# Attention plus gated MLP on one core: PV in batches of eight, zero matmuls at the start, two key segments, denominators by DMA

## The chip, the cores and the metric

The kernel runs on one core of one Trainium2 chip. The metric is device microseconds (us) of an execution. A run of several executions is given as its median. The clock of TensorE in the records is a share of full speed. Only two values of it occur, 0.5 and 1.0, and a mean such as 0.90 says that a fifth of the time was spent at half clock.

On one core a run is labelled slow when it took over 1.5% longer than the fastest run of the same kernel.

Names: TensorE (PE) multiplies matrices, ScalarE (ACT) computes exp and tanh, VectorE (DVE) copies and multiplies elementwise, GpSimd (POOL) does the same more slowly (one layer norm operation of 128x448 takes 1.41 us there and 0.33 us on VectorE, in the profile of before). PSUM is the memory that matmuls write to.

## The reference

```python
# x: 1 x 2048 x 448, bf16; 16 heads of 28; MLP width 1792
xn  = layernorm(x)
qkv = xn @ wqkv                        # 448 x 1344
p   = softmax(q @ k.T * 28**-0.5)      # 16 heads, 2048 x 2048
A   = (p @ v) @ wo
B   = (gelu_tanh(xn @ w_gate) * (xn @ w_up)) @ w_down
out = x + A + B
```

## The kernel before

The scores of one head are computed transposed, keys on partitions. A *unit* is one head, one chunk of 128 keys and one block of 512 queries: one 128x512 score matmul and one PV matmul. There are 4 query blocks x 16 heads x 16 key chunks = 1024 units, three to an exp, so 342 *steps*. Each step emits, in this order, the exp of step p on ScalarE, the three score matmuls of step p+2 on TensorE (two score buffers in PSUM), some PV matmuls, and at most about one *slot*. A slot is a group of four or five matmuls of everything else: projections, V, gate and up, the down and output projections.

```python
spool  = tile_pool(name="spsum",  bufs=2, space=PSUM)   # scores, 3 banks each
otpool = tile_pool(name="otpsum", bufs=1, space=PSUM)   # PV accumulator, 1 bank
aux    = tile_pool(name="aux",    bufs=1, space=PSUM)   # every slot: 1 bank
...
for p in range(NP):                                     # 342 steps
    emit_exp(p)                                         # ScalarE, 128 x 1536
    if tanh_q and tanh_q[0][0] <= p:
        tanh_q.pop(0)[1]()                              # 28 times in all
    if p + 2 < NP:
        emit_s(p + 2)                                   # three score matmuls
    pv_q.extend(units_of(p))
    n = 0
    while pv_q and n < (4 if len(pv_q) > 4 else 3):     # PV: three or four per step
        ...
        emit_pv(pv_q.pop(0)); n += 1
        ...                                             # end of a block: evict, queue g_norm
    ...
    if credit[0] >= 1.0 or due_now or p >= END:
        slots.append(run_slot())                        # one slot
    ...
    for s in evs: s[2]()                                # VectorE empties the slot's bank
```

The softmax denominators come out of the PV matmul as row 0 of each head's 32 rows (V carries a column of ones). Before, they were gathered and spread with matmuls, in 16 normalisations:

```python
def g_norm(Q, hg, otsb, beng=nc.gpsimd):
    ps = aux.tile([P, 16], F32, tag="a", name="dn")
    for ch in range(TPQ):                               # 4 fp32 matmuls, recorded as 8
        nc.tensor.matmul(ps[:, 4*ch:4*ch+4], lhsT=otsb[:, ch*P:(ch+1)*P], rhs=selc[:], ...)
    def f_rec():
        nc.vector.reciprocal(rec[:], ps[:])
        beng.tensor_copy(recx[:], rec[:].unsqueeze(2).to_broadcast([P, 16, 32]))
    yield ("evac", 250, f_rec)
    bt = aux.tile([P, QT], F32, tag="a", name="bt")
    for ch in range(TPQ):
        nc.tensor.matmul(bt[:, ch*P:(ch+1)*P], lhsT=recx[...], rhs=ident[:], ...)
    ...
```

A block runs over all 16 key chunks of four heads, so the first 22 steps already need K and V of every token:

```python
def unit(u):
    return u // 256, (u // 64) % 4, (u // 4) % 16, u % 4   # query block, head group, key chunk, head
```

The softmax here doesn't subtract the row's maximum and nothing guards it: scores larger than these inputs give would overflow.

## Time and profile before

The median is 634.89 us over three runs, 628.87 to 637.83. The profiled execution spans 621.2 us. It is a separate execution of 623.05 us, faster than all of these: the stage table below shows before near its best.

| stage (profile of before) | us | ScalarE's floor | lost |
|---|---|---|---|
| head, until the first exp | 23.2 | | |
| first block, 86 exps | 188.3 | 119.2 | 69 |
| rest, 256 exps | 396.4 | 366.4 | 30 |
| tail, after the last exp | 13.3 | | |

The floor is what ScalarE needs if it never waits. Where exps run back to back in the timeline (near 600 us) they start every 1.342 us, and a tanh adds 0.95 us, so the first block with its four tanh needs 86 x 1.342 + 4 x 0.95 = 119.2 us, and the rest 256 x 1.342 + 24 x 0.95 = 366.4 us.

The page in 40 slices, of before: each digit is the busy share of a slice of 15.5 us in tenths, and PEclk is the granted clock in tenths.

```profile
PE   2477878999989989999999999999898999999874
ACT  1433465869968999999999899998999899999791
PEclk9999996578977999899979799989999799999665
```

ScalarE is nearly full from the fourteenth slice on, and mostly far from full before it.

The busy time of each engine in the four stages, of before. The columns are the stretch in us, its length, the busy time of the five engines with the number of instructions, the mean clock, the DMA share and GB/s.

```profile
0.00:23.20 23.20, 6.91 (x30) 3.18 (x31) 15.08 (x38) 4.70 (x8) 13.07 (x22) 1.00 0.70 173
23.20:211.60 188.40, 159.71 (x827) 50.59 (x826) 70.04 (x129) 125.12 (x92) 40.97 (x62) 0.86 0.10 28
211.60:607.90 396.30, 368.16 (x2361) 129.31 (x2359) 158.56 (x267) 372.38 (x279) 8.43 (x12) 0.93 0.09 27
607.90:621.20 13.30, 5.13 (x20) 2.52 (x16) 4.56 (x8) 0.02 (x1) 0.00 (x0) 0.50 0.10 35
```

The waits of before: who waited for whom, us in total, how often, the longest.

```profile
ACT e L443 <- PE st L429: 86.1, 90, 5.0
...
PE st L429 <- ACT e L443: 18.9, 40, 4.0
...
PE gups L282 <- DVE gu L331: 0.5, 2, 0.2
```

Exps (`e`) wait 86 us for scores (`st`). The view counts waits over 0.15 us.

The timeline of before, one full step in the rest: start in us, duration, engine, line, operation, and in brackets the idle time before it.

```profile
363.71 0.39 PE L429 MATMUL st<-qT,kT_176 28*128 28x512 bf16 x3
...
364.04 0.40 PE L454 MATMUL ot<-e,vaug 128*32 128x512 bf16 x3
...
364.36 0.93 PE L373 MATMUL op<-wd_sb,ht 128*128 128x448 bf16 x4
...
365.23 0.39 PE L429 MATMUL st<-qT,kT_176 28*128 28x512 bf16 x3
```

Score, PV and slot follow each other without a gap: 0.33 + 0.32 + 0.87 = 1.52 us, so this step is longer than the 1.342 us of an exp. Steps with a slot are limited by TensorE, steps without one by ScalarE.

### The profile page before, as it was taken

How to read it: one execution, taken by the hardware profiler on the slowest of the kernel's cores; microseconds unless marked ns; L12 is line 12 of the kernel's file. 1: busy time of each engine (PE TensorE's matmuls, PEld its weight loads, DVE VectorE, ACT ScalarE, POOL GpSimd, SP SyncE). 2: the span in 40 equal slices, each digit the busy share in tenths (PEclk: the TensorE clock that was granted, in tenths of full speed). 3: DMA queues.
4: the chain of work that ended last, by engine and by line, in shares of the span. 5: the costliest groups of instructions: out<-in, count | busy, mean ns of one | idle time of the engine just before them, and what ended most of it. 6: DMA issues, size and time to landing. Idle time of an engine off the chain costs nothing.

```text
span 621.2 us, 7981 instructions
## 1 busy us (share of the span) xinstructions
PE 539.9 (87%) x3232; PEld 185.6 (30%) x3232; DVE 248.2 (40%) x440; ACT 502.2 (81%) x378; POOL 62.5 (10%) x96
## 2 busy tenths in 40 slices
PE   2477878999989989999999999999898999999874
PEld 1122222223322333333333333332332333333321
DVE  6434232045544541155655401656546104650202
ACT  1433465869968999999999899998999899999791
POOL 7586400000000000000000000000000000000000
PEclk9999996578977999899979799989999799999665
DMA  8700000011111100021211001112111002000000
GB/s 205 198 13 0 0 1 2 0 31 30 31 30 31 31 1 16 8 82 46 60 31 31 0 16 46 48 42 60 31 30 31 8 16 61 8 1 1 0 2 30
DMA packets 33925, 20.24 MB, mean 33 GB/s; under 512 B 1568, under 2 KB 33888, under 8 KB 33888
## 3 DMA queue, kind: packets, MB, share of 16 engines
q1 hardware_dynamic: 33088, 18.87, 10.9%
q10 hardware_dynamic: 800, 0.86, 0.5%
q8 instruction: 25, 0.41, 0.3%
q14 instruction: 12, 0.10, 0.1%
HBM read 17.89 MB, written 1.84 MB: 32 GB/s over the span
## 4 chain that ended last, share of the span: by engine, by line
PE 54%; DVE 17%; ACT 17%; issue 9%; POOL 2%; DMA 1%; ACTq 0%; DVEq 0%; POOLq 0%
ACT e L443 15%; PE gups L282 14%; PE st L429 9%; PE ot L454 9%; PE op L373 9%; PE pp L237 5%; DVE gu L331 4%; PE pv L251 3%; PE dn L338 3%; DVE g L293 3%; ACT th L313 2%; DVE vaug L262 2%; DVE res L379 1%; POOL xn L202 1%; DVE qT L244 1%
## 5 line engine op out<-in xcount | busy, mean ns | idle before, releaser
L443 ACT ACTIVATE e<-st 128x1536 bf16<-128x1536 f32 x342 | 474.1, 1459 | 87.2 <-PE st L429 86.1
L454 PE MATMUL ot<-e,vaug 128*32 128x512 bf16 x1024 | 147.5, 434 | 4.4 <-DVE vaug L262 4.4
L282 PE MATMUL gups<-xnT,wg 112*128 112x512 bf16 x224 | 63.9, 412 | 3.9 <-DVE gu L331 0.5
L293 DVE CAST g<-gups 128x512 bf16<-128x512 f32 x56 | 38.7, 691 | 70.2 <-PE gups L282 70.2
L282 PE MATMUL gups<-xnT,wu 112*128 112x512 bf16 x224 | 59.3, 388 | 4.3
L454 PEld LDWEIGHTS <-vaug 128*32 128x32 bf16 x1024 | 34.0, 94 | 94.7 <-issue 83.7
L350 POOL CAST recx<-rec 128x512 bf16<-128x512 f32 x15 | 10.3, 684 | 501.9 <-DVE rec L349 501.9
L373 PE MATMUL op<-wd_sb,ht 128*128 128x448 bf16 x224 | 55.8, 371 | 0.5
L331 DVE TENSOR_TENSOR gu<-gups,g 128x512 bf16<-128x512 f32 x56 | 38.7, 691 | 34.0 <-PE gups L282 33.8
L429 PE MATMUL st<-qT,kT_176 28*128 28x512 bf16 x256 | 39.1, 442 | 8.5 <-ACT e L443 6.0
L429 PE MATMUL st<-qT,kT_179 28*128 28x512 bf16 x256 | 39.9, 438 | 6.9 <-ACT e L443 6.4
L237 PE MATMUL pp<-xnT,wqk_sb 112*128 112x512 bf16 x120 | 38.9, 456 | 5.1 <-DVE xnT L220 1.8
L429 PE MATMUL st<-qT,kT_177 28*128 28x512 bf16 x256 | 38.8, 427 | 3.3 <-ACT e L443 2.8
L429 PE MATMUL st<-qT,kT_178 28*128 28x512 bf16 x256 | 35.3, 394 | 4.6 <-ACT e L443 3.8
L379 DVE TENSOR_TENSOR res<-op,x_sb 128x448 bf16<-128x448 f32 x12 | 7.5, 624 | 70.2 <-PE op L373 70.2
L282 PEld LDWEIGHTS <-wg 112*128 112x128 bf16 x224 | 20.4, 101 | 33.4 <-issue 19.0
L313 ACT ACTIVATE th<-zz 128x1024 bf16<-128x1024 bf16 x28 | 29.7, 1061 | 0.0
L282 PEld LDWEIGHTS <-wu 112*128 112x128 bf16 x224 | 20.0, 98 | 30.7 <-issue 14.0
L373 PEld LDWEIGHTS <-ht 128*128 128x128 bf16 x224 | 19.0, 100 | 25.2 <-issue 14.1
L217 PE MATMUL tp<-ident,xn 128*112 128x128 bf16 x64 | 9.2, 317 | 18.7 <-DVE xn L202 9.8
L338 PE MATMUL dn<-selc,otsb 128*128 128x4 f32 x128 | 18.8, 270 | 7.3 <-DVE otsb L617 5.4
L251 PE MATMUL pv<-wv_sb,xnT 112*128 112x448 bf16 x64 | 21.5, 477 | 2.0 <-DVE kT_176 L244 1.6
(102 smaller groups left out, 353.8 us busy)
## 6 DMA issues: line engine op xcount, KB each, us to landing
wg<-in_B_w_gate_dram SPq DMA_DIRECT2D x28, 224.0 KB
wu<-in_B_w_up_dram SPq DMA_DIRECT2D x28, 224.0 KB
out_dram<-res SPq DMA_DIRECT2D x16, 112.0 KB
wd_sb<-in_B_w_down_dram SPq DMA_DIRECT2D x1, 1568.0 KB
x_sb<-in_A_x_dram SPq DMA_DIRECT2D x2, 448.0 KB
wst<-in_A_wqkv_dram SPq DMA_DIRECT2D x1, 392.0 KB
wst<-in_A_wqkv_dram ACTq DMA_DIRECT2D x1, 392.0 KB
wv_sb<-in_A_wqkv_dram SPq DMA_DIRECT2D x1, 392.0 KB
```

The costliest lines, as they stand in the source:

```text
L237: nc.tensor.matmul(pp[:, 0:QT] if ps is None else pp, lhsT=wqk_sb[:, comp, hg, c, :], rhs=xnT[:, c, T * QT : (T + 1) * QT], start=(c == 0) ...
L251: nc.tensor.matmul(pv[:, 0:D], lhsT=xnT[:, c, tt * P : (tt + 1) * P], rhs=wv_sb[:, c, :], start=(c == 0), stop=(c == NDC - 1),)
L282: nc.tensor.matmul(ps[:], lhsT=w[:, c, k * P : (k + 1) * P], rhs=xnT[:, c, Q * QT : (Q + 1) * QT], start=(c == 0), stop=(c == NDC - 1),)
L293: yield ("evac", C_EVAC, lambda ps=ps, k=k: nc.vector.tensor_copy(g[:, k, :], ps[:]))
L313: nc.scalar.activation(st["t"][:], st["z"][:], AF.Tanh, scale=TANH_SCALE)
L331: yield ("evac", C_EVAC, lambda ps=ps, k=k: nc.vector.tensor_mul(gu[:, k, :], ps[:], g[:, k, :]))
L338: nc.tensor.matmul(ps[:, 4 * ch : 4 * ch + 4], lhsT=otsb[:, ch * P : (ch + 1) * P], rhs=selc[:], start=True, stop=True,)
L373: nc.tensor.matmul(ps[:, 0:D], lhsT=l, rhs=r, start=(first and n == 0), stop=(last and n == len(seq) - 1))
L379: nc.vector.tensor_add(res[:], a, b)
L429: nc.tensor.matmul(st[:, j * QT : (j + 1) * QT], lhsT=kT[hg][32 * hh : 32 * hh + Dh, kc * P : (kc + 1) * P], rhs=qT[(Q, hg)][32 * hh : 32 ...
L443: nc.scalar.activation(e[:, 0:n], st[:, 0:n], AF.Exp, scale=SCALE)
L454: nc.tensor.matmul(ot_cur[0][32 * hh : 32 * hh + 32, :], lhsT=vaug[:, kc, h * 32 : (h + 1) * 32], rhs=e[:, j * QT : (j + 1) * QT], start=( ...
```

## The change

The change has four announced parts, and some smaller ones in the same diff.

1. **PV in batches of eight units.** PV is emitted only when eight units wait, every second or third step. Fewer switches between score and PV matmuls should free TensorE.
2. **Zero matmuls while inputs load.** 24 matmuls of zeros at the start and a few more in the head keep TensorE busy, so that its clock is full when the first real work comes.
3. **First query block in two key segments.** All head groups first run over key chunks 0 to 3, later over 4 to 15, and the partial results are added. The first 21 steps then need only the first four token tiles.
4. **Denominators reshaped by DMA.** Four small DMAs spread row 0 of each head over partitions, VectorE takes the reciprocal, four DMAs bring it back to a row, and one matmul broadcasts it.

Smaller: layer norm of tiles 4 to 15 goes mostly from GpSimd to VectorE and later; its evictions in the head are split; slots are admitted by an estimate of TensorE's backlog; the output stores at the end use two queues. Exp buffers go from 7 to 6.

```diff
-        n = 0
-        while pv_q and n < (4 if len(pv_q) > 4 else 3):
-            ...
+        take = 8 if len(pv_q) >= 8 else (4 if p >= NP - 4 and len(pv_q) >= 4 else 0)
+        if take and unit(pv_q[take - 1])[2] in v_done:
+            for _ in range(take):
+                u = pv_q.pop(0)
+                if emit_pv(u) and u != NU - 1:
+                    close_block(u)
... (cut)
+    SEG = 4
+    blocks = [(0, hg, 0, SEG) for hg in range(NHG)] + [(0, hg, SEG, NKC) for hg in range(NHG)]
+    blocks += [(Q, hg, 0, NKC) for Q in range(1, NQ) for hg in range(NHG)]
... (cut)
+    def norm_stage1(otsb):
+        for j in range(4):
+            nc.sync.dma_start(den[32 * j : 32 * j + 32, :], otsb[32 * j : 32 * j + 1, :])
+    def norm_stage2(den, rr):
+        nc.vector.reciprocal(rec[:], den[:])
+        nc.vector.tensor_copy(recb[:], rec[:])
+        for j in range(4):
+            nc.sync.dma_start(rr[32 * j : 32 * j + 1, :], recb[32 * j : 32 * j + 32, :])
+    def g_norm(Q, hg, otsb, rr):
+        nc.tensor.matmul(bt[:], lhsT=sel[:], rhs=rr[:], start=True, stop=True)
... (cut)
+    def junk(ps, n):
+        for _ in range(n):
+            nc.tensor.matmul(ps, lhsT=zt[:, 0:P], rhs=zt[:], start=True, stop=True)
+    jt = otpool.tile([P, QT], F32, tag="ot", name="jt")
+    junk(jt[:], 24)
... (cut)
+        if overdue or ((credit[0] >= 1.0 or p >= END) and backlog + C_SLOT <= dt + 900):
+            ev = run_slot()
```

## The prediction

> What bounds it now. ScalarE is the long pole, fed by TensorE. By the groups, 342 exps keep ScalarE busy 474 us, 28 tanh 30 us. Back to back, exps start every 1.342 us (timeline, 598-606 us), so ScalarE's floor is 342 x 1.342 + 28 x 0.95 = 485 us; the span is 621 us. The waits show ScalarE idle 86 us for score matmuls. The stretch table places the loss: first exp at 23.2 us; the first query block (86 exps) lasts until about 200 us, where 86 x 1.342 + 7 tanh is 122 us, so 55 us are lost; the other 256 exps take about 408 us against 364, so 44 us are lost; from the last exp to the end pass 13 us.
>
> TensorE causes this twice. Warm, its work nearly fills the time: 342 score groups and 334 PV batches (instruction order) of 3 or 4 matmuls at 0.32 us of issue each (four cost what three cost), about 240 slots of four or five matmuls at 0.97 us, 16 normalisations at 1.4 us: 109 + 108 + 232 + 22 = 470 us. And it is often not warm: the granted clock is 0.5 at 97-131, 178-192, 579-590 and from 597 us, and durations say the start is cold too (four K matmuls 1.86 us at 34 us, 1.02 us at 86 us), though the clock row shows 1.0 there. The cold stretches follow a 4 us slice with TensorE under 60% busy. That agrees with the Trainium skill, "TensorE: Matmul & The Clock Gate", Part 1 (half clock by default and after an idle window of about 3.4 us).
>
> What the change does.
> 1. PV by eight: 128 batches. If the switch costs 0.32 - 0.216 = 0.1 us, eight cost 2 x 0.216 + 0.1 = 0.54 us; 69 us in place of 108.
> 2. Denominators by DMA: 128 small fp32 matmuls (18.8 us busy) and 64 others become 15 single matmuls; about 20 us off TensorE, and its waits for the reciprocal go. The price, eight tiny DMAs per block, hides behind eight steps (11 us).
> Together TensorE falls to about 410 us warm, clearly under ScalarE.
> 3. Zero matmuls should warm TensorE; that and fewer operations before the first exp (layer norm of tiles 4-7 moved out, a split evacuation, earlier table load) bring it to about 16.5 us; the weight DMA at 10.3 us stays the limit.
> 4. Two key segments: the first 21 steps need only token tiles 0-3, so the rest of layer norm, transposes, K and V spreads over the block. Most of the 55 us come back.
> 5. Tail: bf16 denominators, four output banks, two store queues: 3 us less.
>
> Sum: 16.5 + 485 + 10 = 511 us if ScalarE never waited. I allow 28 us of stalls (half in the first block, half from cold stretches) and some 10 us for the clock's phase, since the runs before spread by 9 us.
>
> Predicted: 550 us, range 527 to 585. Faster by over 2%: 0.95; within 2%: 0.03; slower: 0.02.
>
> Right if: first exp before 18 us; 86th exp ends before 155 us; PV batches of eight near 0.54 us at full clock; ScalarE's idle time for score matmuls falls from 86 to under 35 us; TensorE's busy time falls by 60 us or more; ScalarE over 88% busy.
>
> Wrong if: lower TensorE load lets the clock fall to half more often (mean under 0.85), so that slots limit again; zero matmuls don't count as activity; denominator DMAs land later than four steps and block VectorE; the single auxiliary PSUM bank makes slots wait for evacuations; the layer norm of tiles 4-15 comes too late for step 22.

## More of the kernel before

Verdicts use the other runs, the fast ones.

The clock row shows half-clock stretches. Its first record lies at 76.8 us, so the nines before that are not a measurement. The matmuls themselves tell: the same V projection takes 1.68 us before the record and 0.93 us after it (timeline of before).

```profile
68.64 1.68 PE L251 MATMUL pv<-wv_sb,xnT 112*128 112x448 bf16 x4
...
78.25 0.93 PE L251 MATMUL pv<-wv_sb,xnT 112*128 112x448 bf16 x4
```

All matmuls of projection slots from 34.8 to 76.3 us start 0.33 to 0.43 us apart, and those of the first slot after 76.8 us 0.19 to 0.20. So the clock was at half there too, and of the first block not 51 us, as recorded, but some 105 us passed at half clock if the stretch from the first exp to 34.8 us was like the rest.

In the rest both engines are over 90% busy: TensorE 368 and ScalarE 372 of 396 us.

The timeline of before at a normalisation:

```profile
145.82 1.05 PE L338 MATMUL dn<-selc,otsb 128*128 128x4 f32 x8
...
147.23 0.61 POOL L350 CAST recx<-rec 128x512 bf16<-128x512 f32 x1 [48.34 <-DVE rec L349]
...
147.90 0.40 PE L355 MATMUL bt<-ident,recx 128*128 128x128 bf16 x4 [0.38 <-POOL recx L350]
...
149.15 1.89 PE L237 MATMUL pp<-xnT,wqk_sb 112*128 112x512 bf16 x4
```

Right after it, from 148.5 us on, the clock is at half, and the projection slot (`pp`) takes 1.89 us instead of 1.0.

## The result, and the profile after

The changed kernel takes 571.14 us (median of four runs, 566.59 to 577.09). Before, four runs in the same rounds give 635.09 us. The ratio of fast runs is 0.898, with a 95% interval of 0.888 to 0.908. All ratios here are the mean time of one kernel's fast runs over that of the other's fast runs of the same rounds, so they are not quite the ratios of the medians.

The prediction of 550 us lay 21 us low, and the measurement inside its range. The stages below are those of the two profiles.

| stage | before | after | difference |
|---|---|---|---|
| head | 23.2 | 19.0 | -4.2 |
| first block | 188.3 | 142.0 | -46.3 |
| rest | 396.4 | 399.0 | **+2.6** |
| tail | 13.3 | 9.6 | -3.7 |

Between the two profiles, nearly the whole gain lies in the first block. The rest, two thirds of the time, gained nothing, although TensorE is busy 31 us less there. The table accounts for 51.6 of the 64 us between the medians, because the profile of before is of an execution 12 us faster than its median; where the other 12 us lie in a usual run of before is not shown.

The page in slices (14.2 us each), of after:

```profile
PE   7768788878788999888789898878886998869775
ACT  2778879988899899999885999999989899998983
PEclk9998997998999699999875999999986899989977
```

The busy time by stage, of after:

```profile
0.00:19.00 19.00, 14.77 (x67) 5.78 (x68) 14.23 (x42) 5.50 (x9) 11.40 (x30) 1.00 0.97 212
19.00:161.00 142.00, 111.89 (x771) 36.46 (x769) 72.82 (x146) 122.24 (x91) 2.69 (x13) 0.93 0.11 28
161.00:560.00 399.00, 337.18 (x2253) 101.79 (x2252) 167.89 (x293) 371.54 (x280) 0.00 (x0) 0.91 0.11 30
560.00:569.60 9.60, 4.27 (x22) 1.32 (x18) 4.28 (x8) 0.59 (x2) 0.00 (x0) 0.86 0.15 48
```

In the rest TensorE is busy for 337 us in place of 368, but the stretch is as long as before, and its mean clock fell from 0.93 to 0.91.

The waits of after:

```profile
PE st L473 <- ACT e L487: 47.8, 71, 1.9
ACT e L487 <- PE st L473: 41.9, 66, 2.2
...
PE gups L315 <- DVE g L326: 11.9, 27, 0.5
...
PE gups L315 <- DVE gu L365: 7.8, 19, 0.5
```

TensorE now waits 48 us for ScalarE (19 before), and ScalarE still 42 us for TensorE. Each is idle for the other at different times. The last two lines are new: gate and up slots wait 46 times, 19.7 us together, for VectorE to empty their bank.

The timeline of after, one such wait:

```profile
283.76 0.69 DVE L365 TENSOR_TENSOR gu<-gups,g 128x512 bf16<-128x512 f32 x1 [0.39 <-PE gups L315]
284.16 1.45 ACT L487 ACTIVATE e<-st 128x1536 bf16<-128x1536 f32 x1
...
284.51 1.02 PE L315 MATMUL gups<-xnT_187,wu 112*128 112x512 bf16 x4 [0.46 <-DVE gu L365]
...
285.46 0.39 PE L473 MATMUL st<-qT,kT_3_1668 28*128 28x512 bf16 x3
...
285.79 0.40 PE L500 MATMUL ot<-e,va_155 128*32 128x512 bf16 x4
...
285.96 1.45 ACT L487 ACTIVATE e<-st 128x1536 bf16<-128x1536 f32 x1 [0.35 <-PE st L473]
286.01 0.39 PE L500 MATMUL ot<-e,va_156 128*32 128x512 bf16 x4
...
286.33 1.04 PE L270 MATMUL pp<-xnT_188,wqk_sb 112*128 112x512 bf16 x4
```

VectorE empties the bank until 284.45. The slot had stood ready for 0.46 us and starts at 284.51. The scores are queued behind the slot and start at 285.46, and ScalarE idles 0.35 us before the exp that needs them. The two exps start 1.80 us apart, not 1.34: the 0.46 us are passed on. The step before had a slot too and no PV in between; the eight PV matmuls come only afterwards, and take 286.33 - 285.79 = 0.54 us, as predicted.

In the head, the timeline of after shows a tiny operation that takes long:

```profile
6.25 2.41 DVE L192 CAST mvb_191<-mv_190 128x8 bf16<-128x8 f32 x1
...
7.04 1.59 POOL L122 MEMSET wo_sb<- 128x1792 bf16 x1
8.69 0.17 DVE L193 TENSOR_SCALAR ve_192<-mvb_191 128x4 bf16<-128x4 bf16 x1
```

The cast of 128 x 8 elements ends at 8.66 us, when the memset on GpSimd ends (8.63). The next operation, half its size, takes 0.17 us. In the second profile of the same kernel (a_again below) the cast ended before this memset began, and the timeline of a_again shows:

```profile
6.38 0.25 DVE L192 CAST mvb<-mv 128x8 bf16<-128x8 f32 x1
...
7.10 1.59 POOL L122 MEMSET wo_sb<- 128x1792 bf16 x1
```

### The profile page after: what moved, and what is told of

Read it like the earlier page. It is cut to its first block, busy times and chain, and to the rows that moved or that the text cites. A ratio compares the mean times of both kernels' runs of the same rounds, so it can differ in the third digit from the quotient of the medians.

```text
span 569.6 us, 7901 instructions
## 1 busy us (share of the span) xinstructions
PE 468.1 (82%) x3106; PEld 145.3 (26%) x3106; DVE 259.2 (46%) x486; ACT 499.9 (88%) x379; POOL 14.1 (2%) x43
## 4 chain that ended last, share of the span: by engine, by line
PE 44%; ACT 28%; DVE 14%; issue 12%; POOL 0%; DMA 0%; DVEq 0%; ACTq 0%; POOLq 0%
ACT e L487 24%; PE gups L315 14%; PE st L473 8%; PE ot L500 7%; PE op L407 6%; PE pp L270 5%; ACT th L346 3%; DVE gu L365 3%; PE pv L284 3%; DVE g L326 2%; DVE res L413 1%; DVE xn L235 1%; DVE qT L277 0%; DVE on L390 0%; DVE zz L341 0%
## 5 line engine op out<-in xcount | busy, mean ns | idle before, releaser
L487 ACT ACTIVATE e<-st 128x1536 bf16<-128x1536 f32 x342 | 471.1, 1477 | 47.7 <-PE st L473 41.9
L407 PEld LDWEIGHTS <-ht 128*128 128x128 bf16 x224 | 19.2, 100 | 31.3 <-issue 20.5
L519 DVE COPY otsb<-ot 128x512 f32<-128x512 f32 x12 | 8.3, 691 | 32.4 <-PE ot L500 21.3
L331 DVE TENSOR_TENSOR sq<-g 128x1024 bf16<-128x1024 bf16 x28 | 19.3, 688 | 0.4
L357 DVE TENSOR_TENSOR ht<-ph,gu 128x1024 bf16<-128x1024 bf16 x28 | 19.2, 686 | 0.4
L270 PEld LDWEIGHTS <-wqk_sb 112*128 112x128 bf16 x128 | 11.9, 104 | 29.0 <-issue 22.6
L341 DVE TENSOR_TENSOR zz<-po,g 128x1024 bf16<-128x1024 bf16 x28 | 19.2, 684 | 0.3
L315 PE MATMUL gups<-xnT_188,wg 112*128 112x512 bf16 x56 | 16.9, 432 | 2.5 <-DVE g L326 1.2
L390 DVE TENSOR_TENSOR on<-otsb,bt 128x512 bf16<-128x512 f32 x15 | 10.3, 685 | 18.3 <-PE bt L387 18.3
L315 PE MATMUL gups<-xnT_188,wu 112*128 112x512 bf16 x56 | 16.1, 415 | 2.7 <-DVE g L326 1.8
L315 PE MATMUL gups<-xnT_187,wg 112*128 112x512 bf16 x56 | 15.3, 397 | 2.9 <-DVE g L326 1.8
L315 PE MATMUL gups<-xnT_186,wg 112*128 112x512 bf16 x56 | 15.3, 397 | 2.7 <-DVE g L326 1.4
L277 DVE CAST qT<-pp 128x512 bf16<-128x512 f32 x15 | 10.4, 692 | 15.3 <-PE pp L270 15.3
L315 PE MATMUL gups<-xnT_189,wg 112*128 112x512 bf16 x56 | 14.4, 380 | 3.1 <-DVE g L326 1.4
L315 PE MATMUL gups<-xnT_186,wu 112*128 112x512 bf16 x56 | 14.4, 380 | 3.0 <-DVE g L326 1.7
L315 PE MATMUL gups<-xnT_189,wu 112*128 112x512 bf16 x56 | 15.3, 398 | 1.8 <-DVE gu L365 0.9
```

Of the source, the lines that this page charges most:

```text
L270: nc.tensor.matmul(pp[:, 0:QT] if ps is None else pp, lhsT=wqk_sb[:, comp, hg, c, :], rhs=xnT[T][:, c, :], start=(c == 0), stop=(c == NDC ...
L315: nc.tensor.matmul(ps[:], lhsT=w[:, c, k * P : (k + 1) * P], rhs=xnT[Q][:, c, :], start=(c == 0), stop=(c == NDC - 1),)
L331: nc.vector.tensor_mul(st["a"][:], g[:], g[:])
L341: nc.vector.tensor_mul(st["z"][:], st["b"][:], g[:])
L357: nc.vector.tensor_mul(ht[:], st["p"][:], gu[:])
L407: nc.tensor.matmul(ps[:, 0:D], lhsT=l, rhs=r, start=(first and n == 0), stop=(last and n == len(seq) - 1))
```

## The experiments

Twelve runs were made, of ten new kernels and two repeats, all with correct results. Kernels whose name begins with b_ start from the kernel before, those with a_ from the changed one. The two theories on the rest were:

- **Bank:** with PV in every step, its 0.32 us between two slots hid the emptying of the one bank (0.69 us). With eights, a slot often follows a slot directly and must wait.
- **Clock:** with less to do, TensorE has idle moments, the clock falls to half, and slots limit again.

### a_pv4: the changed kernel with PV in threes and fours

```diff
-        take = 8 if len(pv_q) >= 8 else (4 if p >= NP - 4 and len(pv_q) >= 4 else 0)
-        if take and unit(pv_q[take - 1])[2] in v_done:
-            for _ in range(take):
+        n = 0
+        while pv_q and n < (4 if len(pv_q) > 4 else 3):
...
```

> The changed kernel with PV put back to batches of three and four. LOAD expects 20 to 30 us more than the changed kernel (about 595 us), most of it after the first block. STAGE expects at most 10 us more (571 to 581 us), the rest of the exps within 6 us of the 399 us of the changed kernel.

Measured: 559.6 us (552.57 to 569.36), ratio to before 0.882 (0.875 to 0.890). Undoing the part that was meant to relieve TensorE made the kernel faster; both theories for this run expected it slower or the same. The profile is of the fastest of its runs (552.57 us), so it flatters a_pv4. In it the rest takes 381.2 us, 18 less than after, and TensorE is busier in it (348.3 against 337.2 us) at a mean clock of 0.97. The busy time of that stage, and two waits, of a_pv4:

```profile
159.80:541.00 381.20, 348.26 (x2251) 117.36 (x2250) 167.15 (x293) 370.60 (x280) 0.00 (x0) 0.97 0.12 31
```

```profile
PE st L473 <- ACT e L487: 28.8, 55, 1.6
...
PE gups L315 <- DVE gu L365: 0.5, 1, 0.5
```

The timeline of a_pv4, one step with PV between two slots:

```profile
171.42 0.39 PE L473 MATMUL st<-qT,kT 28*128 28x512 bf16 x3
171.52 0.69 DVE L365 TENSOR_TENSOR gu<-gups,g 128x512 bf16<-128x512 f32 x1 [0.52 <-PE gups L315]
...
171.74 0.40 PE L500 MATMUL ot<-e,va 128*32 128x512 bf16 x3
...
172.27 1.02 PE L315 MATMUL gups<-xnT,wg 112*128 112x512 bf16 x4
```

While VectorE empties the bank (171.52 to 172.21), TensorE does scores and then PV, and the slot starts without a wait in the records. In the order of the traces, 120 slots of the changed kernel follow the slot of the step before with no PV in between; in the kernel before and in a_pv4 it is 5. (The expectation of a_mix below has 98 and 3, by a count of its own.) Both theories are still standing: the bank waits went from 19.7 to under 1 us, but the clock rose too.

### a_again and a_pv4_again: both once more, on another chip

No edit.

> The changed kernel itself, unchanged, so that the next three stand beside it on the same chip. 566 to 577 us as before, granted clock about 0.91, about 100 us at half clock.

> The changed kernel with PV in threes and fours, a second time and beside the changed kernel: the first time it was faster (559.6 us; 39.9 us at half clock in its profile against 98.3, PE busy 484 against 468 us). CLOCK theory: less TensorE work leaves idle stretches, the clock falls to half, and the slots that follow run behind; so it is again 1 to 3% faster than the changed kernel, with a clock over 0.94. Rival CHANCE: the two are within 1%, the first comparison was the clock's phase.

Measured: 572.24 us (563.33 to 575.18), ratio 0.901 (0.892 to 0.910), and 565.85 us (557.16 to 571.10), ratio 0.890 (0.882 to 0.898). The order is the same, with a smaller distance, and here the intervals overlap. Over all eight runs of each, whatever their label, the means are 571.1 and 562.6 us, so eights cost 8.5 us.

The profiles of these two fell into runs labelled slow. Compared with each other they show the same as the first pair: the rest takes 397.4 us with eights and 383.3 us with threes and fours. The first block, however, takes 148.0 and 158.4 us, where the first pair had 142.0 and 142.7: in a_pv4_again 65 us of it passed at half clock, in the others 14 to 41. This is most of what makes one run of these two kernels longer than another.

### a_mix: eights, but at most four in a step after a slot

```diff
+        most = 4 if slot_last else 8
+        n = 0
+        if len(pv_q) >= 8 or (pv_q and (slot_last or p >= NP - 4)):
+            while pv_q and n < most:
...
```

This takes the bank wait away by order alone: nearly every slot after a slot gets PV in between (all but 5 in the trace). There are 251 PV batches then, in place of 128.

> The changed kernel with at most four PV matmuls in a step that follows a slot (so that PV stands between two slots), eights elsewhere: 251 PV batches in place of 128 (eights) or 336 (threes and fours). A slot that follows a slot with no PV between: 98 in the changed kernel, 3 here and 3 with threes and fours. BANK theory: slots share one PSUM bank, a slot must wait until VectorE has emptied it; PV used to hide that, batches of eight uncover it (waits of matmuls for VectorE's gate and up evictions 19.7 us in the changed kernel, none with threes and fours), and the scores behind the slot wait too. Then these waits fall below 4 us and the exps after the first block take 378 to 388 us, total 555 to 566 us. CLOCK theory: what hurts is low TensorE load; the load here is only about 11 us above that of eights, so the half clock stays near 100 us and the rest at 393 to 400 us.

Measured: 572.0 us (568.03 to 582.71), ratio 0.910 (0.904 to 0.915). The changed kernel did not run in this call, so only ratios compare, and this one is no better than its 0.898 and 0.901. In the profile the bank waits are nearly gone and the rest takes 386.2 us, 13 less than after. But the first block takes 154.5 us, with a stretch of 31 us at half clock. Two waits of a_mix:

```profile
PE gups L315 <- DVE gu L365: 2.1, 3, 1.1
...
PE gups L315 <- DVE g L326: 0.7, 2, 0.5
```

So the rest came out as the bank theory expected, but the total did not (555 to 566 us), and the half clock stayed near 100 us, as the clock theory expected. In the rest itself 31 us less passed at half clock than in after, so the 13 us are not the bank's alone. What was gained there was lost in the first block, where the clock was low.

### a_warm: eights, with zero matmuls wherever a step has room

```diff
+        fill = (0 if ran else 2) + (0 if dt == T_EXP else 3)
+        if fill and pv_open[0]:
+            for _ in range(fill):
+                nc.tensor.matmul(ot_cur[0][:], lhsT=zt[:, 0:P], rhs=zt[:], start=False, stop=False, ...)
```

Zeros are added to the open PV accumulator, so the result does not change. A step without a slot gets two, a step with a tanh three more.

> The changed kernel, PV in eights, and zero matmuls (128x512, added into the open PV accumulator, which they leave as it is) wherever a step ran no slot (2) or has a tanh (3). CLOCK theory: they keep the clock up, time at half clock falls from 98 to under 40 us, the exps after the first block take 375 to 385 us in place of 399, total 545 to 558 us. Rival BUNCH: batches of eight are slow because 0.54 us of PV in one step holds back scores; then more matmuls make it no faster: 566 to 585 us.

Measured: 565.05 us (563.11 to 568.42), ratio 0.901 (0.894 to 0.907), beside 0.901 for the changed kernel. In the profile the whole rest ran at full clock, and TensorE waited only 12.3 us for ScalarE. But the rest still takes 391.4 us and the bank waits stay at 20 us. The waits and the stage of a_warm:

```profile
PE st L473 <- ACT e L487: 12.3, 27, 1.4
PE gups L315 <- DVE g L326: 12.0, 26, 0.5
...
PE gups L315 <- DVE gu L365: 8.0, 18, 0.5
```

```profile
160.60:552.00 391.40, 356.88 (x2455) 113.22 (x2454) 168.31 (x293) 372.83 (x280) 0.00 (x0) 1.00 0.11 31
```

So the bank waits outlast the half clock. How much of the loss the clock was, this run does not show: its total is above the 545 to 558 us that the clock theory expected, but it does 202 zero matmuls more in the rest, and a_pv4_warm below shows that zeros placed by this rule can themselves cost time.

### What the four profiles say together

a_mix takes away the bank waits, a_warm the half clock, a_pv4 the bank waits and, in its profile, most of the half clock. For each profile, the idle time of ScalarE in the rest was added up from the trace: every gap over 30 ns by the clock at that moment, and at full clock by whether a slot had waited for its bank in the 2.5 us before. A gap at half clock counts as the clock's, whatever came before it. All four are profiles of fast runs.

| ScalarE idle in the rest, us | after | a_mix | a_warm | a_pv4 |
|---|---|---|---|---|
| at half clock | 12.7 | 6.7 | 0 | 1.2 |
| at full clock, after a bank wait | 5.7 | 0.2 | 10.9 | 0 |
| at full clock, other | 9.0 | 8.7 | 7.7 | 9.3 |
| sum | 27.5 | 15.6 | 18.5 | 10.5 |
| the rest, us | 399.0 | 386.2 | 391.4 | 381.2 |
| of it at half clock | 72.8 | 41.5 | 0 | 21.3 |

From after to a_pv4 the idle time falls by 17.0 us, of which 11.5 us were at half clock and 5.7 us came after bank waits. The other gaps differ by 0.3 us. So BUNCH, the rival for a_warm, that eight PV matmuls in one step hold back scores, finds no support here. By this count, clock and bank share the loss by eights in the rest as about two to one. The two slow profiles give 13.1 and 3.9 us at half clock and 6.0 and 0 us after bank waits, so the same picture. It is a count by coincidence in time, not an experiment on each. Whether the bank also feeds the clock, since a wait is idle time of TensorE, is not shown: a_mix passes 41.5 us of the rest at half clock instead of 72.8, but over its four runs the half clock averages 118 us, more than the 102 us of the changed kernel.

The second way to see the clock is over runs. From the mean clock of a run, its time at half clock is 2 x (1 - clock) x span. Over the eight runs of the changed kernel it averages 102 us, over those of a_pv4 70 us, and a line through each eight has a slope of 0.30 and 0.31 us per us, with runs about 1 us off the line. Nearly all of the run-to-run spread of these two kernels is time at half clock. Over 33 runs of the kernel before, whose first part has no clock record, no such line is seen (slope 0.05).

The lines also say something about the bank. At 100 us of half clock they give 570.6 us for the changed kernel, 571.9 for a_pv4 and, through the four runs of a_mix, 568.6. So at the same half clock the three orders of PV take the same time within some 3 us: over the whole kernel, the 8.5 us that eights cost are no more than the 32 us more at half clock (0.30 x 32 = 9.6 us), and the cost of the bank waits, beside what eights save, is too small to see. The lines are not drawn out to zero, where no run of these kernels lies.

### a_pv4_warm: threes and fours, with the same zero matmuls

The edits of a_pv4 and a_warm together.

> PV in threes and fours and the same zero matmuls. CLOCK theory: little half clock is left in this one (40 us), so the gain is small, 0 to 8 us against PV in threes and fours alone, and PV in eights with zero matmuls is the equal of this one or a few us better, as its TensorE has more room at full clock. BUNCH: this one stays 10 us or more ahead of PV in eights with zero matmuls.

Measured: 582.31 us (577.26 to 584.66), ratio 0.925 (0.918 to 0.932), 16 us slower than a_pv4_again beside it. The rest ran at full clock, with no bank wait, and took 403.6 us, because TensorE was now busy for 545 of 583 us. Zero matmuls are real work: where no room is left they hold up the scores. Neither theory foresaw this. A first build of this kernel added zeros to a part of the accumulator that had not been started, and did not go to the chip.

### b_pv8: the kernel before with eights alone

```diff
-        n = 0
-        while pv_q and n < (4 if len(pv_q) > 4 else 3):
...
+        take = 8 if len(pv_q) >= 8 else (4 if p >= NP - 4 and len(pv_q) >= 4 else 0)
+        if take and unit(pv_q[take - 1])[2] in v_done:
...
```

> The kernel before with one thing changed: PV in batches of eight. Two theories. LOAD (the prediction): TensorE's load limits the whole kernel, so about 39 us less PV issue gives 20 to 30 us: ratio to before 0.95 to 0.97, and the 256 exps after the first query block take about 380 us in place of 396. STAGE (read from the two traces: first exp 23.2 to 19.0 us, first block 188.3 to 142.0 us, the rest 396.4 to 399.0 us, tail 13.3 to 9.6 us): behind the first block ScalarE was already within 31 us of its floor, what TensorE saves there becomes idle time and stretches at half clock; ratio 0.98 to 1.01 and the rest stays at 390 to 402 us.

Measured: 616.2 us (614.37 to 620.65), ratio 0.977 (0.971 to 0.982). In the kernel before, eights help a little. By stage of the profile, the first block became 12 us shorter (176.4) and the rest 9 us longer (405.6). In the rest the same bank waits appear (21.0 us, 47 times, for gate and up slots), and 97 us at half clock in place of 57. Why the first block became shorter is open: in this execution the clock rose at 44.6 us, in that of before at 76.8, so that some 46 us less of the first block passed at half clock. At the slope of 0.30 seen above this alone would be 14 us (an estimate).

### b_seg: the kernel before with two key segments alone

```diff
-    def unit(u):
-        return u // 256, (u // 64) % 4, (u // 4) % 16, u % 4
+    blocks = [(0, hg, 0, SEG) for hg in range(NHG)] + [(0, hg, SEG, NKC) for hg in range(NHG)]
+    blocks += [(Q, hg, 0, NKC) for Q in range(1, NQ) for hg in range(NHG)]
...
-            add(due(0, 0, 4 * T) - 4.5, 1, lambda t0=t0: g_transpose(t0))
+            add((16 * T) // 3 - 4.5, 1, lambda t0=t0: g_transpose(t0))
```

For memory and buffers it needs six exp buffers and five for block results, as the changed kernel has. The transposes had to keep their old dates, since the layer norm of before hands its tiles over a small ring; with later dates a first build deadlocked. So this is the segments without the later layer norm.

> The kernel before with the first query block in two key segments alone (its layer norm, transposes and PV batches stay; one exp buffer fewer, two more buffers for the partial sums). If the order of work is what cost 68 us in the first block: first block 150 to 165 us in place of 188, total 600 to 612 us. If the cold clock was the cost and the order only a symptom: first block over 178 us, ratio over 0.98. The first exp stays near 23 us either way.

Measured: 622.8 us (618.6 to 626.28), ratio 0.986 (0.978 to 0.993). The first block takes 180.3 us, 8 less than before, of which 90 us passed at half clock. The segments alone are worth little in this form: it is the branch of the expectation in which the cold clock, and not the order of work, was the cost.

### a_nozero and b_zero: zero matmuls, taken away and given alone

```diff
# a_nozero, from the changed kernel
-    jt = otpool.tile([P, QT], F32, tag="ot", name="jt")
-    junk(jt[:], 24)
-        junk(jt[:], 2)
...
# b_zero, into the kernel before
+    junk(24)
+            junk(4)
+    junk(3)
```

> The changed kernel without the zero matmuls at the start (those of the tail stay). If they are what makes the first block fast: half clock until some tens of us, first exp at 20 to 22 us, first block 155 to 165 us in place of 142, total 585 to 595 us. If TensorE warms by itself once the segments keep it fed: first exp about 20 us, first block within 5 us of 142, total within 6 us of the changed kernel.

> The kernel before with 24 zero matmuls at the start and 11 among its first matmuls. If the cold clock of the first 76 us cost much: first exp at 21.5 to 22.5 us, first block 165 to 175 us in place of 188, total 610 to 620 us. If the first block is bound by layer norm on GpSimd and by one exp at a time waiting for V and K in order: first block over 182 us, ratio over 0.985, and the clock falls again at once.

Measured: a_nozero 580.86 us (580.20 to 581.04), ratio 0.919 (0.915 to 0.923); b_zero 630.11 us (626.17 to 633.37), ratio 1.003 (0.995 to 1.010). Removing the zeros from the changed kernel costs 10 us: the first exp comes at 20.7 us and the first block takes 151.3. The first clock record is a rise at 35.0 us, in place of 5.9 with the zeros, and the slot matmuls before it start 0.33 to 0.43 us apart, at half clock. So 52 us of the first block passed at half clock in place of 20.5, and 31 us more would, at the slope of 0.30 found over runs above, be the 9 us (an estimate). Given to the kernel before, they bring nothing. The first exp comes 1.6 us earlier, but then the clock falls at 20 us and stays at half for 116 us. The first block of b_zero:

```profile
21.60:218.60 197.00, 169.34 (x827) 52.49 (x826) 69.99 (x129) 125.17 (x92) 40.96 (x62) 0.67 0.10 28
```

The zeros give a full clock to the first work, and keep it only if enough work follows at once. In the changed kernel it does.

### a_denmm: the changed kernel with the denominators by matmul again

```diff
+    def g_norm_mm(Q, hg, otsb):
+        for ch in range(TPQ):
+            nc.tensor.matmul(ps[:, 4*ch : 4*ch+4], lhsT=otsb[:, ch*P : (ch+1)*P], rhs=selc32[:], ...)
+        ... nc.gpsimd.tensor_copy(recx[:], rec[:].unsqueeze(2).to_broadcast([P, 16, 32])) ...
     def start_norm(Q, hg, otsb):
+        urgent.append(lambda: g_norm_mm(Q, hg, otsb))
```

To fit and to be free of deadlock it also needed one buffer less for the reciprocals, 16 more slots in the planned count from step 90, and a delay of 12 instead of 9 steps near the end.

> The changed kernel with the denominators by fp32 matmuls and a GpSimd broadcast again, as in the kernel before (scheduling bound for slots kept, last norm as in the changed kernel). In the kernel before, five of its eight falls of the clock after the first block came in the 3.4 us window with these small matmuls. If they cost: 10 to 20 us more than the changed kernel, time at half clock over 120 us. If the DMA path only moved work off a TensorE with room: within 6 us of it.

Measured: 597.64 us (595.7 to 606.0), ratio 0.952 (0.947 to 0.956). The two ratios of the changed kernel are 0.898 and 0.901, so this part is worth some 6% or 26 us, more than any other that was taken out. The medians come from different calls; the cost is above the 10 to 20 us expected. The profile fell into a run labelled slow. In it, 14 of the 16 falls of the clock up to the last exp come within 3.4 us after denominator matmuls; in the kernel before it is 9 of 11. The pattern is that shown for the kernel before: short fp32 matmuls, then often a wait for GpSimd (0.16 to 1.1 us, in 13 of 15 normalisations here and 5 of 15 in the kernel before). The time at half clock is 183 us in the profile and 157 us on average over the runs, 55 more than in the changed kernel, which at the slope of 0.30 would be some 17 of the 26 us (an estimate).

### a_best: what the experiments point to

It is a_pv4, with the memsets out of the way of the first operations, the K eviction taken out of the Q projection's way, and zero matmuls only where the schedule's own estimate shows room:

```diff
+        if pv_open[0]:
+            for _ in range(max(0, min(4, int((dt - backlog - 250) // 216)))):
+                backlog += 216
+                nc.tensor.matmul(ot_cur[0][:], lhsT=zt[:, 0:P], rhs=zt[:], start=False, stop=False, ...)
```

> The changed kernel with PV in threes and fours, a shorter head (zeroing of the output weights on VectorE before the tokens land and a quarter of the V constants after the weight copies, so that GpSimd no longer holds VectorE from 6.3 to 8.6 us; K and Q of the first block into two banks, so that Q does not wait for K's eviction; other constants later) and some 65 zero matmuls only where the schedule's own estimate says that TensorE has caught up. First exp at 14.5 to 16 us in place of 17 to 19 us; half clock under 60 us; first block 140 to 150 us, the rest 378 to 386 us as with threes and fours; total 550 to 560 us, ratio to before 0.87 to 0.89. If the zero matmuls get in the way as they did when given to every step, the rest is over 390 us and the total above 562 us.

Measured: 555.82 us (six runs, 555.46 to 561.22), against a median of 630.87 us for the kernel before beside it. Only one of the runs of before counted as fast, so there is no interval. Its slowest run is faster than every run of the kernel before and of the changed kernel. Whether it beats a_pv4 (552.57 to 571.1) is not shown; it ran alone on another chip, and only its spread is clearly smaller. Its rest is the shortest of all, 378.2 us, with 3.4 us at half clock. The first exp comes at 15.9 us, and the cast of the head takes 0.17 us now. Its first block missed the 140 to 150 us expected, with 41 us at half clock. It gives some back in the tail (13.2 us): eight zero matmuls were emitted after the last exp's scores and held TensorE for some 3 us. Without them it should gain a little more; that was not run.

### All profiles by stage

| kernel | label of the profiled run | head | first block | rest | tail | half clock in all | median us |
|---|---|---|---|---|---|---|---|
| before | fast | 23.2 | 188.3 | 396.4 | 13.3 | 123 or more | 635.1 |
| b_pv8 | fast | 23.6 | 176.4 | 405.6 | 13.3 | 150 | 616.2 |
| b_seg | fast | 24.0 | 180.3 | 402.8 | 13.3 | 170 | 622.8 |
| b_zero | fast | 21.6 | 197.0 | 399.2 | 13.3 | 210 | 630.1 |
| after | fast | 19.0 | 142.0 | 399.0 | 9.6 | 98 | 571.1 |
| a_again | slow | 17.5 | 148.0 | 397.4 | 10.3 | 124 | 572.2 |
| a_nozero | fast | 20.7 | 151.3 | 396.5 | 9.6 | 102 | 580.9 |
| a_pv4 | fast | 17.0 | 142.7 | 381.2 | 9.6 | 40 | 559.6 |
| a_pv4_again | slow | 17.6 | 158.4 | 383.3 | 9.8 | 101 | 565.9 |
| a_mix | fast | 19.0 | 154.5 | 386.2 | 9.6 | 108 | 572.0 |
| a_warm | fast | 17.4 | 143.2 | 391.4 | 9.1 | 8 | 565.1 |
| a_pv4_warm | fast | 17.1 | 151.7 | 403.6 | 10.2 | 29 | 582.3 |
| a_denmm | slow | 18.5 | 160.4 | 415.0 | 10.3 | 183 | 597.6 |
| a_best | fast | 15.9 | 152.0 | 378.2 | 13.2 | 53 | 555.8 |

The half clock in this table is what the records hold. Before the first record (76.8 us in before, 44.6 in b_pv8, 35.0 in a_nozero) the spacing of the slot matmuls shows half clock as well. With it, some 105, 58 and 52 us of their first blocks passed at half clock.

## Why the prediction was right or wrong

**The direction and the sum.** Faster by 10% was measured, and the range held the time. The sum was 16.5 + 485 + 10 = 511 us, plus 28 us of stalls and some 10 us for the clock. The profile has 19.0 + 485.6 + 9.6 = 514 us and 55.4 us of stalls (22.8 in the first block, 32.6 in the rest). The term that was mis-sized is the stalls: 38 us were allowed with the clock's phase, 14 of them in the first block, and 55 came. That the time still fell inside the range is in part luck: of the six marks below four were missed or just missed, the range is 58 us wide, and the part that was to relieve TensorE cost time instead of saving it.

**The step that failed: "Together TensorE falls to about 410 us warm, clearly under ScalarE".** TensorE's busy time did fall, by 72 us over the kernel and by 31 us in the rest. The conclusion, that ScalarE would then not wait, failed. A sum over the kernel says nothing about a single step. With one bank, a slot after a slot waits for VectorE, and PV in every step had hidden that; and the freed time became idle moments in which the clock fell. Both were listed under "wrong if", and were given no us in the sum except the 10 us of phase and half of the stalls. The two pairs of a_pv4 show that the part as a whole costs time here (8.5 us on average). Of its two causes, the half clock accounts for about that much over the runs; the bank waits are seen in the profiles (19.7 us against under 1), but their own cost in time is not separated.

**Eights as such.** "PV batches of eight near 0.54 us at full clock" is right (0.54 us in the timeline shown above). The saving, about 38 us of issue (334 batches of 0.32 us against 128 of 0.54), is there, and brought no time in this form.

**The division of the loss.** The prediction ended the first block at "about 200 us" and gave 55 us of loss to it and 44 to the rest. In the trace of before the 86th exp ends at 211.6, so that 69 us were lost there and only 30 in the rest. This is an error of reading. It gave eights more to gain than there was.

**The first block.** "Most of the 55 us come back" is right in size: 46 us. But the reason given, two key segments, is not shown. The segments alone gave 8 us there, eights alone 12, and taking zeros or the DMA denominators out of the changed kernel costs 9 and, in a slow run, 18 (12 against the slow profile of a_again). What the later layer norm on VectorE does is in none of the runs by itself. The parts were undone one by one for 10 + 26 - 9 = 27 of the 64 us. The remainder, which is segments, layer norm, head and tail together, stays unseparated. What the traces do show is the clock: some 105 us of the first block passed at half clock before and 20.5 after. At the 0.30 us per us seen over runs, 84 us less are about 25 of the 46 us (an estimate). The prediction had seen that the start was cold, but gave the 55 us to the order of work.

**Denominators.** About "20 us off TensorE" was the reason given; taking them back costs 26 us. The size is near, and the mechanism has a second half that the prediction did not name: nearly every fall of the clock in a_denmm comes within 3.4 us of these matmuls. How much of the 26 us each half makes is only estimated (17 us for the clock, above). The fear that VectorE would be blocked by late DMAs came true in small: it waited for `den` six times, 10.7 us in all, the longest 3.0 us, and no run shows a cost of that.

**Zero matmuls.** They do count as activity: with them the clock is at full from 5.9 us on, without them from 35.0 (a_nozero), and in a_warm's profile it was at half for only 8 us of 561. They are worth 10 us in the changed kernel and nothing in the kernel before.

**The head.** Predicted 16.5 us and "the weight DMA at 10.3 us stays the limit". It was 19.0, and 17.5 in the repeat of the same kernel. The difference goes with the cast: in the four profiles with this head in which it took 2.3 to 2.4 us (after, a_nozero, a_mix, a_denmm) the first exp came at 18.5 to 20.7 us, in the five in which it took 0.19 to 0.29 us at 17.0 to 17.6. The Trainium skill, "GPSIMD Engine Reference", Specifications, says that GpSimd shares its SBUF interfaces with VectorE; a cast that ends together with GpSimd's memset agrees with that. In a_best, where the memsets were moved along with other edits of the head, the cast takes 0.17 us and the first exp comes at 15.9 us.

**The tail.** Predicted 3 us less, measured 3.7. The clock was at half for all of the 13.3 us before and for 2.7 us after, so not all of it need be the announced edits.

**The marks set in advance.** First exp before 18 us: missed at 19.0 (17.5 in the repeat). 86th exp before 155 us: missed at 161.0. ScalarE's wait for scores under 35 us: missed at 41.9, from 86.1. TensorE 60 us less busy: met, 539.9 to 468.1. ScalarE over 88% busy: just missed at 87.8%. PV batches of eight at 0.54 us: met. Mean clock under 0.85 would have made it wrong: it was 0.916, from 0.902 before, which counts the unrecorded first 77 us as full and is therefore too high.

**The clock.** The Trainium skill, "TensorE: Matmul & The Clock Gate", Part 1, says that the clock is at half by default and after an idle window of about 3.4 us, and at full after a busy one, with windows of 3413 ns that run freely. The traces agree on the window: every stretch but the last of a trace is a multiple of 3.41 us. Over the windows of all 14 traces from the first exp to the end, with matmuls and weight loads counted as busy, a fall to half follows 90 of 123 windows with TensorE under 65% busy, 44 of 767 at 65 to 90%, 2 of 299 at 90 to 95%, and none of 698 above. A rise follows 124 of 206 windows at 95% or more, and none of 219 below. So in these traces half clock mostly begins after one weak window, and ends only after a full one. A kernel whose TensorE is 82% busy on average, as this one, can fall into it, and comes out only when a window fills, as the slowed work lets it.

**The bank.** The Trainium skill, "Perfetto Trace Analysis", Optimizing Tensor Performance, says that independent groups of matmuls should rotate through different PSUM banks, so that the emptying of one overlaps with the next. The changed kernel shows such waits without it: 19.7 us in gate and up slots, and the gap of 0.35 us before an exp shown above. No run tried a second bank for slots (the kernel gives three to each of two score buffers, one to PV and one to slots). What a_mix and a_pv4 show is that the order of instructions can stand in for it.

## What to carry to other kernels

Before making an operation that sits between two others cheaper or rarer, look at what its time hides: here 0.32 us of PV per step hid the emptying of the only bank (seen as waits in the traces; its own cost in the total was too small to separate). Judge a saving on an engine by the stage and step in which that engine is the limit, not by its sum, and where the saved time only becomes idle TensorE, count the half clock that can follow as a cost (0.30 us for each us at half clock in the kernels fitted here). Read the spacing of matmuls where the clock has no record. Fill idle TensorE with zero matmuls only where the schedule has room: 66 placed by an estimate of the room went with the shortest rest of all, but filling steps by a fixed rule cost 16 us with threes and fours and gained nothing sure with eights.

## What the Trainium skill lacked or had wrong

- "TensorE: Matmul & The Clock Gate", Part 1, gives no busy share at which the clock falls or rises. Here falls follow 90 of 123 windows under 65% busy and none of 698 at 95% or more; rises follow only windows of 95% or more (124 of 206), none of 219 below. These shares come from records whose ends are modelled; with weight loads left out, 2 rises follow windows below 95%.
- The same page speaks of an idle window before a fall, and further on of short idle moments that make the clock swing, again without a share. Here 46 of the 136 falls follow windows that were 65 to 95% busy. In the kernel before, 9 of 11 falls come within 3.4 us after the small fp32 denominator matmuls (128x4 outputs) and their wait. That such matmuls count less than their recorded busy time would explain it, but is not shown.
- The same page does not say whether matmuls of zeros count as activity for the clock gate. Of zeros it says only that they do not trip a limiter of peak current, which is another thing. They do count: without them the clock first rises at 35.0 us in a_nozero, with them at 5.9 us in the changed kernel, and with some 200 more of them in the rest and 60 in the first block, the mean clock of a_warm was 0.98 to 1.00 in its runs, against 0.89 to 0.93 for the changed kernel.
- "Perfetto Trace Analysis", Identifying the Most-Contended Engine, warns that the busy share of matmuls is no good measure of how near TensorE is to its limit. It does not say that relief of a busy TensorE can bring nothing: here it fell from 93% to 85% busy in the rest without any gain in time.
- No page says how much other work must stand between two groups that share one PSUM bank. Here 0.69 us of emptying behind 0.65 us of scores and PV leaves no wait over 0.15 us in nearly all gate and up slots; behind 0.33 us of scores alone it leaves a wait of up to 0.5 us in 46 of them.
